# Cross network, six layers: GpSimd copies the corner weights of layers 1 to 5 behind the first half of layer 0 instead of ahead of it

## The chip, the cores and the metric

The kernel runs on one core of a Trainium2 chip. The metric is the device time in microseconds of one execution; of the kernel before there are three, 146.07, 146.46 and 146.69, median 146.46. A separate execution was profiled. The engines are named as in the profile: PE (matrix products), PEld (its weight loads), DVE (elementwise work, copies), ACT (activations, reads of PSUM), POOL (GpSimd), SP (issues DMAs).

## The reference

```python
# x0: 4096 x 416, ws: 6 x 416 x 416, bs: 6 x 416, all bf16
def reference(x0, ws, bs):
    x = x0
    for l in range(ws.shape[0]):
        x = x0 * (x @ ws[l] + bs[l]) + x
    return x
```

Each layer is a 4096 x 416 by 416 x 416 product, a bias, a product with the input and a sum. A layer needs the whole previous one.

## The kernel before, in words

**Layout.** The 416 features are cut into three blocks of 128 (k on the way in, m on the way out) and a remainder of 32. The 4096 rows of x are cut into two streams s of 2048, and each stream into four groups g of 512 columns. From layer 0 to layer 4 the activations stand transposed: XM[i] holds the three full blocks (128 partitions, 3, 4096), XR[i] the remainder, the four groups of a stream stacked in 4 x 32 partitions. XRx is XR of layer 0 with its two halves of 64 partitions swapped. XM[0] comes straight from DRAM by eight transposing DMAs (`load_x0t`, L78, one for each s and g). XR[0] is made on the chip: `load_xrem` (L83) loads rows into xrem, and `x0_rem` transposes them on DVE (L157), copies them into XR (L158) and into XRx (L161). x0_rem runs three times: for stream 0 it is cut in two halves of partitions, the first copied by DVE, the second (partitions 64 to 127, that is groups 2 and 3) by POOL; stream 1 is copied by DVE.

**Weights.** WM holds the rows of the three full blocks, WR the 32 remainder rows (four times, one for each group), WD the corner, remainder rows by remainder columns, laid out as four blocks of a diagonal, zero elsewhere. WD is zeroed by POOL and filled by `fill_wd(l0, l1)`: four POOL copies out of WR (L124). It is called for layer 0 and then for layers 1 to 5. WR of layers 1 to 5 comes by four DMAs of SP (L86).

**Order.** The program's order is written by hand, and each engine executes its own instructions in order. SP's queue holds, in order: the x transposes with the xrem loads among them, WM of layer 1, the four WR loads, WM of layers 2 to 5, X0rows, and later the transposes and stores of the end. Layer 0 is `first_layer(s)`, first s = 0, then s = 1. In it h = 0 (groups 0, 1) and h = 1 (groups 2, 3) come one after the other: 18 full products (L215), the remainder rows (`row`, L222, from XR or XRx), then for each m one tile of elementwise work (`ew_main`: ACT adds the bias out of PSUM, L166; DVE multiplies, L167, and adds, L168). The last part of stream 1 also makes the 32 remainder columns of both streams (`rem_first`: L192 with WD, L197 with WM, then ACT L172 and DVE L173 and L174, one remainder per stream).

Layers 1 to 4 go through six tiles (s, m). PE does 48 quarter products (L180) of the first tile, then the remainder rows of this and the next tile (`mm_row`, L186, which read the XR that the layer before has made), then the other tile's 48, and then, once per layer, `rem_pair`, both streams' remainder columns (L192, L197). Layer 5 is turned around, so that its result has rows on the partitions (L332, L341, L346), and is stored from there.

PSUM is handed out in four pairs of banks in turn (`two_banks`), and ACT's results go through six buffers t.

Of the kernel before, what the change touches and what calls it, by code (L numbers as in the profile page):

```python
# [16 lines left out]
def kernel(  # L17
# [9 lines left out]
    L = ws.shape[0]  # L27
# [42 lines left out]
    def col0(s, g):  # L70
        return SW * s + CW * g
# [50 lines left out]
    def fill_wd(l0, l1):  # L122
        for g in range(NG):
            nc.gpsimd.tensor_copy(WD[32 * g:32 * g + 32, l0:l1, g, :], WR[32 * g:32 * g + 32, l0:l1, NK * P:D])  # L124

    fill_wd(0, 1)
    fill_wd(1, L)

    PS = psum.tile([P, 8, CW], FP32)
    turn = [0]  # L130
# [1 line left out]
    def two_banks():  # L132
        i = 2 * (turn[0] % 4)
        turn[0] += 1
        return PS[:, i:i + 2, :]
# [20 lines left out]
    def x0_rem(s, p0, p1, eng):  # L156
        nc.vector.transpose(out=xrt[s][p0:p1], in_=xrem[s][p0:p1])  # L157
        eng.tensor_copy(XR[0][p0:p1, CW * s:CW * s + CW].rearrange("p (j t) -> p j t", t=16),  # L158
                              xrt[s][p0:p1].rearrange("p t j -> p j t"))
        for a in range(p0, p1, 64):  # L160
            eng.tensor_copy(XRx[s][64 - a:128 - a, :], XR[0][a:a + 64, CW * s:CW * s + CW])  # L161

    def ew_main(l, s, m, h, pt, cur, nxt):
        c0 = col0(s, 2 * h)
        t = tpool.tile([P, 2 * CW], BF16, name="t")
        nc.scalar.activation(t[:], pt.rearrange("p a b -> p (a b)"), ACT.Identity, bias=bM[:, m, l:l + 1], scale=1.0)  # L166
        nc.vector.tensor_tensor(out=t[:], in0=t[:], in1=XM[0][:, m, c0:c0 + 2 * CW], op=ALU.mult)  # L167
        nc.vector.tensor_tensor(out=nxt[:, m, c0:c0 + 2 * CW], in0=t[:], in1=cur[:, m, c0:c0 + 2 * CW], op=ALU.add)  # L168
# [40 lines left out]
    def first_layer(s):  # L209
        cur, nxt = XM[0], XM[1]  # L210

        def full(pt, m, h, gl, first, last):
            c0 = col0(s, 2 * h + gl)
            for k in range(NK):
                nc.tensor.matmul(pt[:, gl, :], lhsT=WM[:, 0, k, 128 * m:128 * m + 128], rhs=cur[:, k, c0:c0 + CW],  # L215
                                 start=(first and k == 0), stop=(last and k == NK - 1), skip_group_check=True)

        def row(pt, m, h, swapped, first):
            for gl in range(2):
                r0 = 32 * ((2 * h + gl + 2 * swapped) % 4)  # L220
                src = XRx[s][r0:r0 + 32, :] if swapped else XR[0][r0:r0 + 32, CW * s:CW * s + CW]
                nc.tensor.matmul(pt[:, gl, :], lhsT=WR[r0:r0 + 32, 0, 128 * m:128 * m + 128], rhs=src,  # L222
                                 start=first, stop=(not first), tile_position=(r0, 0), skip_group_check=True)

        pa = [two_banks() for m in range(NK)]
        if s == 0:
            for gl in range(2):
                for m in range(NK):
                    full(pa[m], m, 0, gl, True, False)
        else:  # L230
            for m in range(NK):
                for gl in range(2):
                    full(pa[m], m, 0, gl, True, False)
        pb = [two_banks()]
        row(pa[0], 0, 0, 0, False)
        row(pa[1], 1, 0, 1, False)
        row(pa[2], 2, 0, 0, False)
        if s == 1:
            row(pb[0], 0, 1, 0, True)
        if s == 0:  # L240
            x0_rem(0, 64, 128, nc.gpsimd)
        for m in range(NK):
            ew_main(0, s, m, 0, pa[m], cur, nxt)
        for gl in range(2):
            full(pb[0], 0, 1, gl, s == 0, s == 1)
        if s == 1:
            ew_main(0, s, 0, 1, pb[0], cur, nxt)
        for m in range(1, NK):
            pb.append(two_banks())
            for gl in range(2):  # L250
                full(pb[m], m, 1, gl, True, False)
        if s == 0:
            row(pb[0], 0, 1, 0, False)
            row(pb[2], 2, 1, 1, False)
            row(pb[1], 1, 1, 0, False)
            x0_rem(1, 0, 128, nc.vector)
            for m in range(NK):
                ew_main(0, s, m, 1, pb[m], cur, nxt)
        else:
            row(pb[1], 1, 1, 0, False)  # L260
            row(pb[2], 2, 1, 1, False)
            rem_first(pb)
# [16 lines left out]
    def rem_first(pb):  # L279
        pr2 = two_banks()  # L280
        for s in range(NS):
            mm_rem(0, s, pr2[:, s, :], XM[0], XR[0])
        for s in range(NS):
            ew_rem(0, s, pr2[:, s, :], XR[0], XR[1])
            ew_main(0, 1, 1 + s, 1, pb[1 + s], XM[0], XM[1])

    first_layer(0)
    first_layer(1)
    cur, curR = XM[1], XR[1]
    for l in range(1, LL):  # L290
# [136 lines left out]
```

## Time and profile before

| | before |
|---|---|
| timed, median of 3 | 146.46 us |
| the profiled execution's own time | 147.55 us |
| its span, first to last instruction | 145.7 us |
| PE busy | 126.2 us, 87% |
| DVE busy | 110.7 us, 76% |
| ACT busy | 83.9 us, 58% |
| POOL busy | 6.7 us, 5% |
| mean granted clock of PE | 0.946 |

The span leaves out 1.85 us around the first and last instruction. Busy shares are means over the whole span; the slices of the profile's page show that PE is at work nearly everywhere from slice 8 on and idle in slices 5 to 8 (some 15 to 29 us), and that its granted clock is low just there and a little beyond. Names in the rows: `t<-PS,bM` reads "writes t, reads PS and bM"; `x18` is a group of 18 merged instructions; a bracket gives the idle time before and what ended it.

### The profile page before, as it was taken

The numbers are of one execution on the slowest core, as the hardware profiler recorded it, in microseconds if no ns is written. First come the engines' busy times: TensorE is split into PE (matmuls) and PEld (weight loads), VectorE is DVE, ScalarE is ACT, GpSimd is POOL, SyncE is SP. The second block draws the span as 40 slices with busy tenths as digits, with TensorE's granted clock in tenths as the row PEclk, the third lists the DMA queues.
The fourth block names the chain that finished last, engine by engine and source line by source line (L and its number), as shares of the span: only waits on it lengthen the run. The fifth ranks groups of instructions, "written<-read, shape, count | busy, mean of one in ns | idle before, by whom it ended". The sixth has DMA issues, their size and how long they took to land.

```text
span 145.7 us, 3943 instructions
## 1 busy us (share of the span) xinstructions
PE 126.2 (87%) x1683; PEld 55.3 (38%) x1683; DVE 110.7 (76%) x196; ACT 83.9 (58%) x92; POOL 6.7 (5%) x20
## 2 busy tenths in 40 slices
PE   6999200199999999999999999999999999999960
PEld 2344000033444444444444445444444444455420
DVE  1256450064699989898988989898898999999990
ACT  1208000080968937759395686759584686675860
POOL 4200000600000000000000000000000120000000
PEclk9999985557999999999999999999999999999997
DMA  4999999999900000000000000000019798997553
GB/s 112 242 196 171 143 222 227 289 331 334 281 10 7 0 4 0 4 0 7 0 4 0 4 0 4 0 4 0 4 25 159 173 164 184 171 302 239 178 193 102
DMA packets 42021, 16.37 MB, mean 112 GB/s; under 512 B 30826, under 2 KB 42004, under 8 KB 42004
## 3 DMA queue, kind: packets, MB, share of 16 engines
q1 hardware_dynamic: 40504, 15.70, 49.3%
q10 hardware_dynamic: 1500, 0.42, 1.4%
q8 instruction: 13, 0.21, 0.6%
q14 instruction: 4, 0.03, 0.1%
HBM read 6.15 MB, written 3.41 MB: 66 GB/s over the span
## 4 chain that ended last, share of the span: by engine, by line
PE 75%; SPq 13%; DMA 4%; POOL 2%; DVE 1%; issue 1%; ACT 0%; DVEq 0%; POOLq 0%
PE PS L180 44%; SPq L78 11%; PE PS L332 11%; PE PS L215 7%; PE PS L186 4%; PE PS L197 4%; DMA WR<-in_ws_dram 4%; PE PS L192 2%; PE PS L341 1%; PE PS L222 1%; PE PS L346 1%; SPq L83 1%; DVE t L367 1%; POOL XR L158 1%; SPq L86 1%
## 5 line engine op out<-in xcount | busy, mean ns | idle before, releaser
L166 ACT ACTIVATE t<-PS,bM 128x1024 bf16<-128x1024 f32 x60 | 62.1, 1114 | 47.1 <-PE PS L222 25.8
L180 PE MATMUL PS<-XM,WM 128*32 128x512 bf16 x1152 | 65.2, 379 | 0.0
L167 DVE TENSOR_TENSOR t<-t,XM 128x1024 bf16<-128x1024 bf16 x60 | 41.5, 692 | 17.7 <-ACT t L166 17.7
L168 DVE TENSOR_TENSOR XM<-t,XM 128x1024 bf16<-128x1024 bf16 x60 | 41.8, 697 | 3.5
L180 PEld LDWEIGHTS <-WM 128*32 128x32 bf16 x1152 | 29.7, 97 | 33.8 <-issue 5.1
L215 PE MATMUL PS<-XM,WM 128*128 128x512 bf16 x72 | 18.9, 423 | 0.0
L332 PE MATMUL PS<-WM,XM 128*128 128x416 bf16 x96 | 17.9, 340 | 0.0
L222 PE MATMUL PS<-XR,WR 32*128 32x512 bf16 x16 | 2.8, 434 | 13.4 <-POOL XR L158 13.4
L356 ACT CAST t<-PS 128x832 bf16<-128x832 f32 x12 | 10.2, 852 | 5.0 <-PE PS L332 2.5
L332 PEld LDWEIGHTS <-XM 128*128 128x128 bf16 x96 | 8.9, 98 | 8.7 <-issue 2.2
L215 PEld LDWEIGHTS <-WM 128*128 128x128 bf16 x72 | 7.5, 107 | 11.2 <-issue 5.3
L197 PE MATMUL PS<-XM,WM 128*32 128x512 bf16 x120 | 8.2, 379 | 0.0
L172 ACT ACTIVATE t<-PS,bR 128x512 bf16<-128x512 f32 x10 | 6.8, 694 | 1.4 <-PE PS L197 1.4
L358 DVE TENSOR_TENSOR o<-t,XLrows 128x832 bf16<-128x832 bf16 x12 | 7.1, 592 | 0.5
L186 PE MATMUL PS<-XR,WR 32*128 32x512 bf16 x96 | 7.3, 379 | 0.0
L357 DVE TENSOR_TENSOR t<-t,X0rows 128x832 bf16<-128x832 bf16 x12 | 7.0, 584 | 0.0
L222 PEld LDWEIGHTS <-WR 32*128 32x128 bf16 x24 | 0.6, 93 | 15.6 <-issue 15.6
L139 PE MATMUL PS<-warm 128*128 128x512 bf16 (+1 forms) x12 | 5.1, 594 | 1.2 <-DVE warm L89 1.2
L276 POOL COPY XLrows<-scrR 128x512 bf16<-128x512 bf16 x2 | 1.4, 714 | 87.2 <-DMA scrR<-XR 87.2
L157 DVE STREAM_TRANSPOSE xrt<-xrem 64x512 bf16<-64x512 bf16 (+1 forms) x3 | 2.1, 708 | 3.6 <-DMA xrem<-in_x_dram 3.6
L174 DVE TENSOR_TENSOR XR<-t,XR 128x512 bf16<-128x512 bf16 x10 | 4.3, 426 | 0.8
L366 ACT CAST t<-PS 128x416 bf16<-128x416 f32 x8 | 4.0, 505 | 1.0 <-PE PS L332 0.8
(37 smaller groups left out, 40.6 us busy)
## 6 DMA issues: line engine op xcount, KB each, us to landing
X0rows<-in_x_dram SPq DMA_DIRECT2D x4, 832.0 KB, 10.0
out_dram<-o SPq DMA_DIRECT2D x12, 208.0 KB, 2.2
WM<-in_ws_dram SPq DMA_DIRECT2D x5, 312.0 KB
out_dram<-o SPq DMA_DIRECT2D x8, 104.0 KB, 2.0
WR<-in_ws_dram SPq DMA_DIRECT2D x4, 130.0 KB, 5.8
WM<-in_ws_dram ACTq DMA_DIRECT2D x1, 312.0 KB, 3.4
XM<-in_x_dram SPq DMA_TRANSPOSE x8, 4.7
xrem<-in_x_dram SPq DMA_DIRECT2D x1, 128.0 KB
```

The source lines that it names most:

```text
L78: nc.sync.dma_start_transpose(out=XM[0][:, :, c0:c0 + CW], in_=x0[c0:c0 + CW, 0:NK * P])
L166: nc.scalar.activation(t[:], pt.rearrange("p a b -> p (a b)"), ACT.Identity, bias=bM[:, m, l:l + 1], scale=1.0)
L167: nc.vector.tensor_tensor(out=t[:], in0=t[:], in1=XM[0][:, m, c0:c0 + 2 * CW], op=ALU.mult)
L168: nc.vector.tensor_tensor(out=nxt[:, m, c0:c0 + 2 * CW], in0=t[:], in1=cur[:, m, c0:c0 + 2 * CW], op=ALU.add)
L180: nc.tensor.matmul(pts[g // 2][32 * q:32 * q + 32, g % 2, :], lhsT=WM[:, l, k, 128 * m + 32 * q:128 * m + 32 * q + 32], rhs=cur[:, k, c0:c ...
L186: nc.tensor.matmul(pts[g // 2][:, g % 2, :], lhsT=WR[32 * g:32 * g + 32, l, 128 * m:128 * m + 128], rhs=curR[32 * g:32 * g + 32, CW * s:CW ...
L197: nc.tensor.matmul(pr[32 * g:32 * g + 32, :], lhsT=WM[:, l, k, NK * P:D], rhs=cur[:, k, c0:c0 + CW], start=False, stop=(k == NK - 1), tile ...
L215: nc.tensor.matmul(pt[:, gl, :], lhsT=WM[:, 0, k, 128 * m:128 * m + 128], rhs=cur[:, k, c0:c0 + CW], start=(first and k == 0), stop=(last ...
L332: nc.tensor.matmul(py[g // 2][:, g % 2, 0:D], lhsT=cur[:, k, q_cols(q, g)], rhs=WM[:, l, k, :], start=(first and k == 0), stop=((not first ...
L356: nc.scalar.copy(tv, py[h][:, :, 0:D])
L357: nc.vector.tensor_tensor(out=tv, in0=tv, in1=X0rows[:, b0:b0 + 5:4, :], op=ALU.mult)
L358: nc.vector.tensor_tensor(out=o[:], in0=tv, in1=XLrows[:, b0:b0 + 5:4, :], op=ALU.add)
```

## The change

The call `fill_wd(1, L)` is taken from its place right behind `fill_wd(0, 1)` and put between `first_layer(0)` and `first_layer(1)`. Since each engine executes in the order of the program, the four POOL copies now stand behind the two POOL copies that `x0_rem` makes inside `first_layer(0)`. All lines below the removed one are numbered one lower in the changed kernel until the inserted line: L158 becomes L157, L192 becomes L191.

```diff
     fill_wd(0, 1)
-    fill_wd(1, L)
 
     PS = psum.tile([P, 8, CW], FP32)
...
     first_layer(0)
+    fill_wd(1, L)
     first_layer(1)
```

On POOL, in the kernel before, from the fill of layer 0's corner on (32x5x32 are the copies of layers 1 to 5, the names behind "waits" are semaphores, DMAHW those of transfers):

```order
11 L124 COPY WD<-WR 32x32 [waits DMAHW4_49,Pool_49]
12 L124 COPY WD<-WR 32x32 [waits DVE_49] x3
13 L124 COPY WD<-WR 32x5x32 [waits DMAHW7_49]
14 L124 COPY WD<-WR 32x5x32 [waits DMAHW0_49]
15 L124 COPY WD<-WR 32x5x32 [waits DMAHW1_49]
16 L124 COPY WD<-WR 32x5x32 [waits DMAHW2_49]
17 L158 COPY XR_96<-xrt_89 64x512 [waits DVE_49,Pool_49]
18 L161 COPY XRx_91<-XR_96 64x512 [waits Pool_49]
```

The same place on POOL in the changed kernel:

```order
11 L124 COPY WD<-WR 32x32 [waits DMAHW4_49,Pool_49]
12 L124 COPY WD<-WR 32x32 [waits DVE_49] x3
13 L157 COPY XR_96<-xrt_89 64x512 [waits DVE_49,Pool_49]
14 L160 COPY XRx_91<-XR_96 64x512 [waits Pool_49]
15 L124 COPY WD<-WR 32x5x32 [waits DMAHW7_49]
16 L124 COPY WD<-WR 32x5x32 [waits DMAHW0_49,Pool_49]
17 L124 COPY WD<-WR 32x5x32 [waits DMAHW1_49]
18 L124 COPY WD<-WR 32x5x32 [waits DMAHW2_49]
```

The copies into XR and XRx, which wait for DVE alone, have moved ahead of the four that wait for transfers. PE's instructions stand in the same order as before; only its waits differ. At layer 1's `rem_pair` PE had, before:

```order
502 L180 MATMUL PS<-XM_94,WM 32x512
503 L192 LDWEIGHTS WD
504 L192 MATMUL PS<-XR_97,WD 32x512 [waits Activation_49]
505 L192 LDWEIGHTS WD
506 L192 MATMUL PS<-XR_97,WD 32x512
```

and has now:

```order
502 L179 MATMUL PS<-XM_94,WM 32x512
503 L191 LDWEIGHTS WD [waits Pool_49]
504 L191 MATMUL PS<-XR_97,WD 32x512 [waits Activation_49]
505 L191 LDWEIGHTS WD [waits Pool_49]
506 L191 MATMUL PS<-XR_97,WD 32x512
```

Each of the four weight loads out of WD waits for its POOL copy there. Layer 0's own weight loads out of WD wait for nothing new.

## Rows read from the trace of the kernel before

**Rows 1.** Timeline of PE: start us, duration us, instruction, [idle before <- releaser].

```profile
11.20 4.16 PE L215 MATMUL PS<-XM,WM 128*128 128x512 bf16 x18
28.72 0.61 PE L222 MATMUL PS<-XR,WR 32*128 32x512 bf16 x2 [13.36 <-POOL XR L158]
```

**Rows 2.** Timeline of POOL, the same columns, 25 to 30 us.

```profile
25.34 0.31 POOL L124 COPY WD<-WR 32x160 bf16<-32x160 bf16 x1 [18.29 <-DMA WR<-in_ws_dram]
...
27.26 0.32 POOL L124 COPY WD<-WR 32x160 bf16<-32x160 bf16 x1 [0.30 <-DMA WR<-in_ws_dram]
27.64 1.03 POOL L158 COPY XR<-xrt 64x512 bf16<-64x512 bf16 x1
28.73 0.61 POOL L161 COPY XRx<-XR 64x512 bf16<-64x512 bf16 x1
```

**Rows 3.** Chain of waits in order of time: start us, us, what.

```profile
11.44 2.07 SPq L78
...
17.14 1.79 SPq L78
...
36.73 3.99 PE PS L215 x18
40.72 0.33 PE PS L222 x4
...
42.89 2.59 PE PS L180 x48
45.48 0.54 PE PS L186 x8
```

**Rows 4.** The x transposes, line 78: issue to landing.

```profile
DMA to landing us min/median/max: 4.6/4.7/4.9
```

**Rows 5.** The WR loads, line 86: issue to landing.

```profile
DMA to landing us min/median/max: 5.7/5.8/6.0
```

**Rows 6.** Timeline of DVE, 10 to 48 us.

```profile
10.38 0.71 DVE L157 STREAM_TRANSPOSE xrt<-xrem 64x512 bf16<-64x512 bf16 x1 [0.91 <-DMA xrem<-in_x_dram]
...
18.16 0.71 DVE L157 STREAM_TRANSPOSE xrt<-xrem 128x512 bf16<-128x512 bf16 x1 [1.84 <-DMA xrem<-in_x_dram]
...
19.53 0.61 DVE L161 COPY XRx<-XR 64x512 bf16<-64x512 bf16 x2
...
37.70 0.69 DVE L167 TENSOR_TENSOR t<-t,XM 128x1024 bf16<-128x1024 bf16 x1 [3.11 <-ACT t L166]
...
43.01 0.42 DVE L173 TENSOR_TENSOR t<-t,XR 128x512 bf16<-128x512 bf16 x1
43.47 0.43 DVE L174 TENSOR_TENSOR XR<-t,XR 128x512 bf16<-128x512 bf16 x1
...
46.65 0.69 DVE L168 TENSOR_TENSOR XM<-t,XM 128x1024 bf16<-128x1024 bf16 x1
```

**Rows 7.** Windows: length, PE, PEld, DVE, ACT, POOL busy, PEclk, DMA share, GB/s.

```profile
15.40:20.00 4.60, 0.00 (x0) 0.00 (x0) 2.62 (x6) 0.00 (x0) 0.00 (x0) 1.00 0.91 138
20.00:22.00 2.00, 0.00 (x0) 0.00 (x0) 0.14 (x1) 0.00 (x0) 0.00 (x0) 0.69 1.17 258
...
34.00:36.00 2.00, 2.00 (x9) 0.74 (x7) 0.59 (x1) 0.00 (x0) 0.00 (x0) 0.90 1.13 336
```

**Rows 8.** Timeline of DVE in layer 4, 116 to 119 us.

```profile
116.32 1.10 DVE L167 TENSOR_TENSOR t<-t,XM 128x1024 bf16<-128x1024 bf16 x1
117.53 1.02 DVE L168 TENSOR_TENSOR XM<-t,XM 128x1024 bf16<-128x1024 bf16 x1
118.47 0.68 DVE L167 TENSOR_TENSOR t<-t,XM 128x1024 bf16<-128x1024 bf16 x1
```

**Rows 9.** Timeline of POOL in the same stretch.

```profile
116.06 0.82 POOL L276 COPY XLrows<-scrR 128x512 bf16<-128x512 bf16 x1 [86.72 <-DMA scrR<-XR]
117.39 0.61 POOL L276 COPY XLrows<-scrR 128x512 bf16<-128x512 bf16 x1 [0.51 <-DMA scrR<-XR]
```

**Rows 10.** DVE's waits from 45 us to the end: total us, times, longest.

```profile
DVE t L167 <- ACT t L166: 3.0, 10, 0.4
```

## The prediction

> **What bounds the kernel now.** I read the PE timeline first, because PE has the largest busy share and an idle stretch there is the first thing to price. In its two rows PE finishes 18 matmuls of layer 0 at 11.20 + 4.16 = 15.36 us, then stands still for 13.36 us until a GpSimd copy into XR (L158) is done [rows 1]. These are the remainder rows of stream 0's second half. The second view, POOL's timeline, says why that copy was late: it needs only the DVE transpose that ended at 10.38 + 0.71 = 11.09 [rows 6], but POOL executes in order, and ahead of it stand four copies into WD that wait for the WR transfers of layers 1 to 5; the last starts at 27.26, so the XR copy starts at 27.64 and XRx is ready at 28.73 + 0.61 = 29.34 [rows 2]. The third view, the chain, carries on from there on PE alone: first layer, then layer 1, whose remainder rows (L186) start at 45.48 [rows 3]. The fourth, the windows, shows the second price of the wait: the granted clock was 1.00 in 15.4 to 20.0 although PE did nothing, 0.69 in 20 to 22, and still 0.90 in 34 to 36, after work had resumed at 28.72 [rows 7]. 1.00 is the 2.4 GHz level; the lower one, 1.2 GHz, reads 0.50.
>
> From the chain view on, PE is never idle until the tail, so whatever moves the L186 at 45.48 moves the end, as long as DVE keeps up. I use that instruction as the milestone.
>
> **What the change does to POOL.** It removes nothing and adds nothing: four copies of 0.31 to 0.32 us [rows 2] go behind two copies (1.03 and 0.61). After it, XR's copy starts when DVE's transpose ends at 11.09, and both are done at about 11.1 + 1.03 + 0.61 + 0.1 = 12.8, some 2.6 us before PE wants them at 15.4. The 13.36 us wait goes whole. The four WD copies issue no DMA and are passed by no queue but POOL's; their transfers are issued by SP, whose order is untouched, so they stay where they are, at 25.3 to 27.6, plus what DVE costs them. The new order makes layer 1's corner matmuls (L191 of the changed kernel) wait for POOL. Behind them on PE stands all of layer 1; they come 3 us after the milestone, so they are late only if the copies are (first rival).
>
> **What is late next: PE's own path.** Matmuls at the full clock go at 3.99/18 = 0.222 us, the rows in 0.54 [rows 3].
> - Rows of stream 0, second half: 15.4 to 15.9.
> - Stream 1, first half, 18 matmuls. The fourth needs x columns whose transpose SP issues at 11.44; these transposes land 4.6 to 4.9 us after issue [rows 4], so at 16.3, before 15.9 + 0.67 = 16.6. No wait; done at 15.9 + 3.99 = 19.9.
> - Its rows need DVE's XRx copies, ended at 19.53 + 0.61 = 20.14 [rows 6]: 20.2 to 20.7.
> - Second half: three matmuls to 21.4, then the last transpose, issued at 17.14 [rows 3], at 22.0; I have no row of its own landing. Fifteen more: 22.0 + 3.33 = 25.3.
> - Rows and corner remainder 42.89 - 40.72 = 2.17, to 27.5; then 48 matmuls of layer 1, 2.59, to 30.1. Layer 1's weights are issued at 17.14 + 1.79 = 18.93; their landing too is unshown, and by WR's 5.7 to 6.0 [rows 5] it is an estimated 24.9, early enough. WR itself is there at 27.2.
>
> So PE could reach the milestone at 30.1. It had the low clock for part of that work before; now its longest pause is under 1 us, so I take the full clock.
>
> **DVE's path is longer by a little.** The milestone reads stream 0's remainder of layer 0, which DVE makes. DVE waits for the second xrem transfer until 18.16, which no part of the change touches, and ends its layout copies at 20.14. Behind them stand three tiles of stream 0 (four took 43.01 - 37.70 = 5.31, so 1.33 each, 3.98), then the piece that ran from 37.70 to 43.47 + 0.43 = 43.90, 6.20 [rows 6]. ACT feeds these in time: past 45 us, where DVE works at the same pace, it waited for ACT 3.0 us in all [rows 10]. Sum: 20.14 + 3.98 + 6.20 = 30.32, with a handover 30.4. DVE ends the wait, not PE. Without any disturbance the milestone moves from 45.48 to 30.4: 15.1 us.
>
> **The disturbance.** Before, DVE was idle while POOL copied into WD; now DVE is in its multiply and add tiles. The only rows with both at work are near the end: two POOL copies of 0.82 and 0.61 [rows 9] lie beside a multiply of 1.10 and an add of 1.02, where the next multiply has 0.68. That tile took 118.47 - 116.32 = 2.15 instead of 1.33 [rows 8], so 0.82 for 1.43 us of copies, 0.57 per us. For 4 x 0.315 = 1.26 us this is 0.72. The bounds are 0, if the copies fall between, and 0.41 per copy whatever its length, 1.64. I take 0.72, since the copies are short. The earlier pair at 11 to 13 us costs nothing: DVE waits for xrem anyway (1.84 us idle before 18.16).
>
> The Trainium skill speaks of this under "SBUF — State Buffer", section "SBUF: two separate sides": GpSimd and a VectorE instruction with two SBUF inputs lock one shared pair of ports for a whole instruction, and the other one waits entirely. By that the four copies could cost 1.26 and the gain would be 13.8; the trace agrees that DVE is stretched, though by 0.41 beside a copy of 0.82.
>
> Milestone: 30.4 + 0.72 = 31.1, a shift of 45.48 - 31.1 = 14.4. Is DVE then able to follow? It ends layer 0 at 46.65 + 0.69 = 47.34 before, 3.44 after the remainder's end, so at 30.32 + 0.72 + 3.44 = 34.5 now. PE needs this for stream 1's corner remainder of layer 1, at 31.1 + 0.54 + 2.59 + 0.92 = 35.2 (0.92 is stream 0's half of 2.17 - 0.33): spare 0.7. DVE's shift is 12.8, so it trails PE by 1.6 more than before, and it has 3.0 us of waiting for ACT left in ten pieces up to the end [rows 10] to catch up in. PE therefore keeps the 14.4.
>
> **Sum.** The profiled execution took 147.55 us, span 145.7 and 1.85 around it; it lies 1.09 above the median of 146.46. 147.55 - 14.4 = 133.15 for it, and 146.46 - 14.4 = 132.1 for the median, which I predict. The forecast's own range: port cost 0 gives 131.4, port cost 1.64 gives 146.46 - 13.4 = 133.1; with half a us for run to run and small waits, 130.8 to 133.6.
>
> **Rivals.**
> - POOL is locked out. From 18.16 on DVE works almost without a pause; if the WD copies get in only when it stops, PE meets its new wait at 30.4 + 0.54 + 2.59 = 33.5. DVE finishes what it has: layer 0 at 33.8 and four tiles, 39.1; then four copies, about 1.3 to 1.9. PE goes on at 40.7, 7.2 late: 146.46 - 15.1 + 7.2 = 138.6. For it: DVE's chain above has no gap. Against it: at 116.06 and 117.39 POOL's copies did run beside DVE's tiles and took 0.82 and 0.61 [rows 8, 9]. 6%. The skill's exclusive lock on that page is the rule from which such a lockout would come.
> - A transfer takes the wait's place. Everything PE asked for after 28 us had long landed, so late landings don't show in the waits. Were the last transpose as late as WR (27.2), the milestone would come at 27.2 + 3.33 + 2.17 + 2.59 = 35.3, 4.2 later: 136.3. Against it: transposes have landed in 4.6 to 4.9. 8%, spread between 133 and 137.
> - Slower than before: the clock. The small waits on x could leave PE at half rate from about 21 us on, as it was in 22 to 34 before. Each us of full-speed work then costs one more, so from 14.4 us of such work on, some 8 us into layer 1, the kernel is slower than before; 20 us of it would give 146.46 - 14.4 + 20 = 152.1. Against it: the clock stayed 1.00 through 4.6 us of idleness and was back at 0.90 in 34 to 36, within 8 us of the work's return at 28.72 [rows 1, 7]. 2%.
> - The order on POOL does not matter, as XR would be held up by another wait on its way, its time staying at 146.5. Its only input was there at 11.09. 2%.
>
> **Chances.** The forecast has 82%. The range 130.8 to 134.8 holds it and part of the transfer case. About 0.5% of the time, 0.7 us, is what a measurement can tell from no change: faster 0.96 (forecast, lockout, transfer), same 0.02, slower 0.02.
>
> **What would show it.** Right: XR's POOL copy starts near 11.2; no PE wait above 1.5 us before layer 1; the granted clock stays 1.00 in 15 to 35; DVE runs gapless from 18.2 to beyond 34; the first L185 stands near 31 and is released by DVE's remainder add; the tiles beside the WD copies are stretched by 0.7 in sum. Wrong: an L191 of layer 1 released by POOL (lockout), an L214 released by a DMA for more than 1 us (transfer), clock under 0.9 after 20 (clock), or idle PE in layers 2 to 4, which would mean that DVE did not catch up.

## The result and the profile after

| | before | changed |
|---|---|---|
| timed, median | 146.26 us (145.95 to 146.69, 4 runs) | 132.75 us (132.46 to 132.90, 4 runs) |
| ratio to before | | 0.907, 95% interval 0.904 to 0.910 |
| profiled execution, its span | 147.55, 145.7 us | 132.90, 131.1 us |
| PE busy, mean granted clock | 126.2 us, 0.946 | 122.8 us, 0.991 |
| DVE busy | 110.7 us | 111.2 us |
| POOL busy | 6.7 us | 8.3 us |

The changed kernel is 13.5 us faster by the medians and 14.65 by the two profiled executions. The profiled execution of before is a slow one: it lies 1.29 us above this median, at a mean clock (0.946) that its fast runs have too (0.943 to 0.964 in the sets below), so the 14.65 is not the gain of the median. POOL's timeline of the changed kernel answers to [rows 2]:

```profile
11.21 1.03 POOL L157 COPY XR<-xrt 64x512 bf16<-64x512 bf16 x1 [4.29 <-DVE xrt L156]
12.31 0.96 POOL L160 COPY XRx<-XR 64x512 bf16<-64x512 bf16 x1
25.03 0.31 POOL L124 COPY WD<-WR 32x160 bf16<-32x160 bf16 x1 [11.77 <-DMA WR<-in_ws_dram]
25.83 2.29 POOL L124 COPY WD<-WR 32x160 bf16<-32x160 bf16 x3 [0.49 <-DMA WR<-in_ws_dram]
```

XR's copy starts at 11.21 instead of 27.64 and waits for DVE, its only input. The WD copies stand where they stood (25.03 for the first, 25.34 before), but three of them fill 2.29 us. PE's timeline, against [rows 1]:

```profile
12.61 3.40 PE L214 MATMUL PS<-XM,WM 128*128 128x512 bf16 x14 [1.20 <-DMA XM<-in_x_dram]
15.94 0.39 PE L221 MATMUL PS<-XR,WR 32*128 32x512 bf16 x2
...
27.35 2.76 PE L179 MATMUL PS<-XM,WM 128*32 128x512 bf16 x48
30.84 0.61 PE L185 MATMUL PS<-XR,WR 32*128 32x512 bf16 x8 [0.73 <-DVE XR L173]
...
33.98 0.39 PE L191 MATMUL PS<-XR,WD 128*32 128x512 bf16 x4
```

The 13.36 us wait for POOL is gone. What is left are 1.20 us for an x transpose and 0.73 for DVE's remainder add ahead of the first L185; layer 1's L191, which now waits for POOL too, has no idle time before it. The first L185 stood at 45.48 before [rows 3], so it moved by 14.64, and the span shrank by 14.6: nothing was given back later. DVE's timeline, against [rows 6], shows the new pace maker:

```profile
11.63 1.16 DVE L166 TENSOR_TENSOR t<-t,XM 128x1024 bf16<-128x1024 bf16 x1 [0.55 <-ACT t L165]
12.83 0.98 DVE L167 TENSOR_TENSOR XM<-t,XM 128x1024 bf16<-128x1024 bf16 x1
...
18.44 0.71 DVE L156 STREAM_TRANSPOSE xrt<-xrem 128x512 bf16<-128x512 bf16 x1 [1.97 <-DMA xrem<-in_x_dram]
...
25.81 0.68 DVE L166 TENSOR_TENSOR t<-t,XM 128x1024 bf16<-128x1024 bf16 x1
26.53 0.69 DVE L167 TENSOR_TENSOR XM<-t,XM 128x1024 bf16<-128x1024 bf16 x1
27.14 0.80 DVE L166 TENSOR_TENSOR t<-t,XM 128x1024 bf16<-128x1024 bf16 x1
...
30.36 0.42 DVE L173 TENSOR_TENSOR XR<-t,XR 128x512 bf16<-128x512 bf16 x1
```

From the second xrem transpose at 18.44 to the remainder add's end at 30.78 no row of DVE carries an idle time. The windows (columns as in [rows 7]) show that the clock no longer falls in this stretch. First one of before, where it read 0.50, then those of the changed kernel:

```profile
28.00:34.00 6.00, 5.22 (x16) 1.70 (x16) 3.39 (x6) 3.12 (x3) 1.27 (x2) 0.50 1.11 331
```

```profile
20.00:22.00 2.00, 1.87 (x15) 0.51 (x14) 1.90 (x5) 1.10 (x2) 0.00 (x0) 1.00 1.14 253
...
28.00:34.00 6.00, 5.27 (x100) 2.37 (x96) 5.83 (x11) 4.72 (x6) 0.12 (x1) 1.00 1.11 331
34.00:36.00 2.00, 2.00 (x44) 1.01 (x40) 1.97 (x4) 2.00 (x4) 0.00 (x0) 1.00 1.11 333
```

One caution on the chain view after. It names a transfer as what came before a DVE multiply:

```profile
22.22 6.36 DMA WM<-in_ws_dram
...
28.59 0.69 DVE t L166
```

That multiply reads no weights, and DVE came to it straight from the add before it. The link is inferred, and wrong; the timeline of DVE corrects it.

### The profile page after: what moved, and what is told of

It is laid out like the page before. It is cut to its first block, busy times and chain, and to the rows that moved or that the text cites. A ratio compares the mean times of both kernels' runs of the same rounds, so it can differ in the third digit from the quotient of the medians.

```text
span 131.1 us, 3942 instructions
## 1 busy us (share of the span) xinstructions
PE 122.8 (94%) x1681; PEld 54.5 (42%) x1683; DVE 111.2 (85%) x196; ACT 84.0 (64%) x92; POOL 8.3 (6%) x20
## 4 chain that ended last, share of the span: by engine, by line
PE 72%; SPq 16%; DMA 5%; DVE 3%; issue 1%; ACT 0%; DVEq 0%
PE PS L179 46%; SPq L78 13%; PE PS L332 12%; PE PS L185 5%; DMA WM<-in_ws_dram 5%; PE PS L196 4%; PE PS L341 2%; SPq L86 1%; PE PS L191 1%; PE PS L346 1%; SPq L83 1%; DVE t L367 1%; SPq L74 1%; DVE o L370 1%; DVE t L166 1%
## 5 line engine op out<-in xcount | busy, mean ns | idle before, releaser
L166 DVE TENSOR_TENSOR t<-t,XM 128x1024 bf16<-128x1024 bf16 x60 | 42.1, 702 | 2.4 <-ACT t L165 2.4
L179 PEld LDWEIGHTS <-WM 128*32 128x32 bf16 x1152 | 29.7, 97 | 33.8 <-issue 5.1
L214 PE MATMUL PS<-XM,WM 128*128 128x512 bf16 x70 | 16.4, 379 | 1.4 <-DMA XM<-in_x_dram 1.2
L214 PEld LDWEIGHTS <-WM 128*128 128x128 bf16 x72 | 6.8, 97 | 10.6 <-issue 3.2
L185 PE MATMUL PS<-XR,WR 32*128 32x512 bf16 x96 | 7.3, 379 | 0.7 <-DVE XR L173 0.7
L196 PEld LDWEIGHTS <-WM 128*32 128x32 bf16 x120 | 3.2, 97 | 3.2
L102 DVE COPY WR<-WR 32x416 bf16<-32x416 bf16 x3 | 0.8, 260 | 4.4 <-DMA WR<-in_ws_dram 4.3
```

The lines of the kernel that those rows point to most:

```text
L179: nc.tensor.matmul(pts[g // 2][32 * q:32 * q + 32, g % 2, :], lhsT=WM[:, l, k, 128 * m + 32 * q:128 * m + 32 * q + 32], rhs=cur[:, k, c0:c ...
L185: nc.tensor.matmul(pts[g // 2][:, g % 2, :], lhsT=WR[32 * g:32 * g + 32, l, 128 * m:128 * m + 128], rhs=curR[32 * g:32 * g + 32, CW * s:CW ...
L196: nc.tensor.matmul(pr[32 * g:32 * g + 32, :], lhsT=WM[:, l, k, NK * P:D], rhs=cur[:, k, c0:c0 + CW], start=False, stop=(k == NK - 1), tile ...
```

## The experiments

The runs come in three sets; those of one set share a chip and the runs of the kernel before. Before had a median of 145.39 (144.77 to 147.04) in the first, 146.02 (144.79 to 146.95) in the second and 145.78 (145.07 to 147.82) in the third, 11 runs each.

### POOL's order alone: DVE makes the copies (first set)

```diff
 # kernel before
-            x0_rem(0, 64, 128, nc.gpsimd)
+            x0_rem(0, 64, 128, nc.vector)
```

> The kernel before with one word changed: the second half of stream 0's remainder is copied into XR and XRx by DVE instead of POOL; the four WD copies of layers 1 to 5 stay in their old place. Theory (PE waited only because XR's copy stood behind WD's on POOL): PE's 13.4 us wait goes as fully as in the changed kernel, since DVE has the 0.9 us for the two copies free ahead of its xrem wait; 132.4 to 133.1 us, first L186 of layer 1 at 30.5 to 31.1. Rival (the gain hangs on something else that moving the WD copies does, such as when they read WR): the time stays near 146.

Measured: 132.30 us (132.11 to 132.44), ratio to before 0.908 (0.903 to 0.913), a little below the 132.4 to 133.1 expected, as is the first L186 at 30.19 (30.5 to 31.1 expected). PE's and POOL's rows, in the line numbers of before:

```profile
30.19 0.61 PE L186 MATMUL PS<-XR,WR 32*128 32x512 bf16 x8 [1.00 <-DVE XR L174]
```

```profile
23.53 0.31 POOL L124 COPY WD<-WR 32x160 bf16<-32x160 bf16 x1 [16.52 <-DMA WR<-in_ws_dram]
24.77 1.97 POOL L124 COPY WD<-WR 32x160 bf16<-32x160 bf16 x3 [0.93 <-DMA WR<-in_ws_dram]
```

With the WD copies in their old place on POOL and XR's copy off POOL, the same time is reached: the changed kernel's ratio is 0.907 (0.904 to 0.910). So the gain comes from XR's copy no longer standing behind WD's; anything else that the move does is within the half per cent of these intervals.

### The clock's share: fillers in the wait (first and second set)

```diff
 # kernel before, first_layer(0); 60 and 54 matmuls
         if s == 0:
+            for i in range(60):
+                nc.tensor.matmul(PS[:, 4, :], lhsT=warm[:, 0:P], rhs=warm[:], start=True, stop=True, skip_group_check=True)
             row(pb[0], 0, 1, 0, False)
```

> The kernel before with 60 more matmuls of 512 columns on constant data (result unused) ahead of the remainder rows for which PE waits; the wait on POOL stays. It prices the clock alone. Theory: the granted clock stays 1.00, the rows still start at 28.7 to 29.4, and PE's work from 29.4 to 45.5 shrinks to 0.33+3.99+0.54+3.99+2.17+2.59 = 13.6, so the first L186 comes at 43.0, 2.5 earlier, and the profiled execution at 145.0; since nothing is left that varies with the clock, the timed runs agree with the profiled one, 144.6 to 145.2. Rival A (the profiled execution of before lies 1.1 above its median for another reason): the median is 146.3 - 2.5 = 143.8. Rival B (low clock cost nothing): 146.3.

> The kernel before with 54 instead of 60 filler matmuls ahead of the remainder rows that wait for POOL. With 60 the fillers themselves ended at 28.0, after XRx at 27.9, so they ended the wait. With 54 they end near 26.9, PE waits some 1 us for POOL again, with the granted clock at 1.00. Theory: from XRx's end to the first L186 13.9 to 14.0 us instead of the 16.1 of before, so the low clock costs 2.1 to 2.2 us; time 143.2 to 144.3, at or below the 144.2 of the 60. Rival (the low clock is worth only the 1.2 us by which the 60 fillers changed the median): equal to 144.2 or above.

Measured: 144.23 us (143.91 to 144.29) with 60 and 144.33 (143.69 to 145.37) with 54; ratios to before 0.990 (0.984 to 0.995) and 0.990 (0.984 to 0.996). With 60 the fillers were still running when XR was ready: the rows started at 28.03 without a wait, while XR's copy had ended at 26.22 + 1.04 = 27.26. So the 60 spoil part of what they show. With 54, PE waits for POOL again, and the clock is 1.00 (PE timeline, then windows):

```profile
28.94 0.39 PE L222 MATMUL PS<-XR,WR 32*128 32x512 bf16 x2 [1.70 <-POOL XR L158]
...
43.22 0.61 PE L186 MATMUL PS<-XR,WR 32*128 32x512 bf16 x8
```

```profile
22.00:28.00 6.00, 5.24 (x25) 2.25 (x23) 0.00 (x0) 0.00 (x0) 1.39 (x5) 1.00 1.15 243
28.00:34.00 6.00, 4.79 (x28) 1.95 (x31) 3.38 (x6) 3.12 (x3) 1.49 (x2) 1.00 1.11 332
```

From the rows' start to the first L186 are 43.22 - 28.94 = 14.28 us. The same timeline of before has that row at

```profile
45.41 0.61 PE L186 MATMUL PS<-XR,WR 32*128 32x512 bf16 x8
```

which is 45.41 - 28.72 = 16.69 us behind its rows [rows 1]. The low clock cost 2.4 us in the profiled execution of before, where 2.1 to 2.2 were expected. By the medians the fillers gain 1.69, interval 0.5 to 2.4, so whether the timed runs pay the same is left open within that: the 144.33 lies just outside the theory's 143.2 to 144.3 and fits its rival (144.2 or above), and only the trace decides for the theory. The expectation's theory for the 60 (144.6 to 145.2) missed: it took the profiled execution's arrival of WR (XR's copy at 27.64, here at 26.22), which is the next point.

### Whom the kernel before waits for: WR earlier (second set)

```diff
 # kernel before, SP's queue
+    for g in range(NG):
+        load_wr(nc.sync, g, 1, L)
     load_x0t(1, 2)
     load_x0t(1, 3)
     load_wm(nc.sync, 1)
-    for g in range(NG):
-        load_wr(nc.sync, g, 1, L)
```

> The kernel before with SP's four WR loads issued ahead of stream 1's last two x transposes instead of behind layer 1's weights; POOL's order is as before. Theory (the kernel before hands on the landing of WR one for one, through POOL's order): WR is issued 5.4 us earlier and lands 5 to 5.5 us earlier, so XR's copy on POOL and PE's rows come 5 to 5.5 us earlier, and the clock falls for a shorter time or not at all; 138.5 to 141 us. Rival (POOL's own start, the x transposes or layer 1's weights release PE): 144 or more.

Measured: 139.92 us (139.34 to 140.01), ratio 0.958 (0.953 to 0.964). PE's timeline, then POOL's:

```profile
21.46 0.61 PE L222 MATMUL PS<-XR,WR 32*128 32x512 bf16 x2 [5.91 <-POOL XR L158]
...
37.29 0.61 PE L186 MATMUL PS<-XR,WR 32*128 32x512 bf16 x8
```

```profile
20.00 0.32 POOL L124 COPY WD<-WR 32x160 bf16<-32x160 bf16 x1 [0.20 <-DMA WR<-in_ws_dram]
20.39 1.03 POOL L158 COPY XR<-xrt 64x512 bf16<-64x512 bf16 x1
```

POOL's order is as before, and XR's copy comes 27.64 - 20.39 = 7.25 us earlier because WR does, more than the 5 to 5.5 expected, since WR also landed 3.4 us after its issue instead of 5.7 to 6.0 [rows 5]. The span is 8.2 shorter (137.5); most of the rest is the stretch from the rows to the first L186, 37.29 - 21.46 = 15.83 against 16.69. So the kernel before hands on WR's arrival to its end. That arrival differs between executions: XR's copy began at 27.64 in the profile of before, 26.22 with the 60 fillers and 27.86 with the 54, in which nothing ahead of it on POOL is changed.

### The changed kernel again, as a base (second and third set)

> The changed kernel once more, as the base for the other runs of this call. 132.3 to 132.9 us; first L185 of layer 1 released by DVE's remainder add after a PE wait of 0.5 to 1.1 us. If the kernel before varies more from execution to execution than this one, because it alone hands on how late the WR transfers land, its times spread over 1.5 to 2.3 us in this call and these over less than 0.8.

> The changed kernel as the base for the other two runs of this call, on the same chip: 131.7 to 132.9 us, PE's wait for DVE ahead of the first L185 0.5 to 1.1 us.

Measured: 132.09 us (131.70 to 132.52; 132.3 to 132.9 expected) and 132.12 (131.69 to 132.65), 6 runs each; ratios 0.905 (0.900 to 0.910) and 0.906 (0.903 to 0.910). PE's wait for DVE ahead of the first L185 was 1.03 and 0.68. The spread is 0.8 and 1.0 us, that of before 2.2 and, without its longest run, 1.9 in the same sets. That is what a kernel that no longer waits for WR would show, but not proof: before has more runs, and the kernel with WR earlier, which still waits for it, spread over 0.7 in four.

### What the WD copies cost DVE: left out (first and third set)

```diff
 # changed kernel
     first_layer(0)
-    fill_wd(1, L)
     first_layer(1)
```

> The changed kernel without the four WD copies of layers 1 to 5 (WD stays zero there, so the corner products are left out of the result). It prices what these copies cost DVE. Theory from the trace after: DVE loses some 0.2 us beside them (its path from the second xrem transpose to the remainder add took 12.34 instead of 12.16), so the first L185 comes 0.1 to 0.3 earlier and the time is 132.4 to 132.7. Rival (the predicted 0.72 was right and is hidden in the trace): 132.0. Rival (PE's new wait in layer 1 for POOL costs something): PE's idle time ahead of L191 of layer 1 in the changed kernel goes here, and the time falls by as much.

> The changed kernel without the four WD copies of layers 1 to 5 (their corner products are left out of the result), now beside the base on one chip. Theory (these copies cost DVE 0.15 to 0.36 us, as the paths of 12.35 to 12.56 against 12.20 say): 0.1 to 0.5 us under the base. Rival (the predicted 0.72): 0.7 or more under it.

Measured: 131.72 us (131.51 to 132.15) without a base beside it, below all that was expected, and 132.10 (131.57 to 132.40) beside the base's 132.12, where 0.1 to 0.5 less were expected. The medians show no difference, and with spreads of 0.8 to 1.0 us they can't show one of 0.2. The trace is sharper. From the second xrem transpose's start to the end of stream 0's remainder add, DVE took 12.20 us without the copies in both profiles, and 12.34, 12.55 and 12.44 in the three profiles of the changed kernel: 0.14 to 0.35 more, on average 0.24. These are DVE's rows without them:

```profile
17.25 0.71 DVE L156 STREAM_TRANSPOSE xrt<-xrem 128x512 bf16<-128x512 bf16 x1 [1.14 <-DMA xrem<-in_x_dram]
...
29.03 0.42 DVE L173 TENSOR_TENSOR XR<-t,XR 128x512 bf16<-128x512 bf16 x1
```

The predicted 0.72 is out. PE had no idle time ahead of layer 1's L191, with or without the copies, so the new wait for POOL costs nothing.

### Whether DVE sets the pace: xrem earlier, and off SP (first and second set)

```diff
 # changed kernel, first variant
+    load_xrem(nc.sync, 1, 0, 128)
     load_x0t(1, 1)
-    load_xrem(nc.sync, 1, 0, 128)
 # changed kernel, second variant: both loads of SP's queue go to ACT's
     load_xrem(nc.scalar, 0, 0, 64)
+    load_xrem(nc.scalar, 0, 64, 128)
+    load_xrem(nc.scalar, 1, 0, 128)
```

> The changed kernel with the second stream's xrem load issued by SP one place earlier, ahead of stream 1's second x transpose. Theory (DVE's path from the second xrem landing decides when layer 1's remainder rows start): xrem lands 2 us earlier, at about 16.4, DVE starts its layout copies at 16.5 behind stream 0's first tiles, and the remainder add is done near 28.9; PE's own path, 30.1, then decides, and PE's 0.73 us wait ahead of the first L185 goes: L185 at 30.1 to 30.3, 132.0 to 132.2 us. Rival (PE's path decides, through the x transposes, and the wait for DVE is only its shadow): unchanged or up to 0.6 later, since the second transpose of stream 1 moves 0.6 back: 132.7 to 133.3.

> The changed kernel with the two xrem loads of SP's queue moved to ACT's queue, right behind the first one. Theory (after the change the first layer is paced by what SP issues one after the other: the x transposes for PE, the second xrem for DVE): the last x transpose is issued 1.3 us earlier, near 15.8, and lands near 20.6; the second xrem is there before DVE has finished stream 0's first tiles at 16.5; first L185 at 28.9 to 29.5 and 131.0 to 131.6 us. Rival (the DMA engines, whose busy share is 0.9 to 1.3 in 4 to 16 us, are the limit and not SP): the 64 byte rows of xrem go ahead of the x transposes, stream 0 starts later by their time, and the total is 132.3 to 134.

Measured, first variant: 132.65 us (132.16 to 133.11), ratio to before 0.911 (0.906 to 0.916), no base in its set. PE's timeline:

```profile
17.49 3.40 PE L214 MATMUL PS<-XM,WM 128*128 128x512 bf16 x15 [0.68 <-DMA XM<-in_x_dram]
...
30.12 0.61 PE L185 MATMUL PS<-XR,WR 32*128 32x512 bf16 x8
```

The wait for DVE is gone, as the theory says, and the first L185 stands at the 30.1 of PE's own path; but PE pays 0.68 for the transpose that was moved back, as the rival says, and the time does not fall. Second variant: 131.91 us (131.71 to 131.96) beside 132.09, not the 131.0 to 131.6 expected. Again DVE is early and PE late, now at its start:

```profile
8.93 2.10 PE L214 MATMUL PS<-XM,WM 128*128 128x512 bf16 x9 [0.84 <-DMA XM<-in_x_dram]
...
29.81 0.61 PE L185 MATMUL PS<-XR,WR 32*128 32x512 bf16 x8
```

So the two paths, DVE's through xrem and PE's through the x transposes, lie about a microsecond apart (PE waits 0.68 to 1.03 us in the three profiles of the changed kernel), and moving a transfer trades one for the other.

### A version meant to beat both: a tile into DVE's idle time (third set)

```diff
 # changed kernel, first_layer(0)
-            x0_rem(1, 0, 128, nc.vector)
             for m in range(NK):
                 ew_main(0, s, m, 1, pb[m], cur, nxt)
+                if m == 0:
+                    x0_rem(1, 0, 128, nc.vector)
```

> The changed kernel with DVE's layout copies for stream 1 placed behind the first tile of stream 0's second half instead of ahead of all three. Theory (DVE stands idle 1.5 to 2.0 us for the second xrem with a tile ready behind it, and its path decides when layer 1's remainder rows start): the tile fills the idle time, the copies start at 18.1 to 18.4 instead of 17.9, two tiles instead of three stand behind them, the remainder add is done 0.8 to 1.1 us earlier, PE's wait ahead of the first L185 falls to 0 to 0.3, and the time is 0.6 to 1.0 us under the base. Rival (PE's rows of stream 1, which wait for these copies, are what matters): they start 0.3 later, and the time is equal to the base within 0.3.

Measured: 131.37 us (131.01 to 132.06) beside the base's 132.12, 0.75 less; ratio to before 0.902 (0.898 to 0.906) against the base's 0.906 (0.903 to 0.910). DVE's timeline, then PE's:

```profile
17.00 0.69 DVE L166 TENSOR_TENSOR t<-t,XM 128x1024 bf16<-128x1024 bf16 x1 [0.38 <-ACT t L165]
...
18.33 0.70 DVE L156 STREAM_TRANSPOSE xrt<-xrem 128x512 bf16<-128x512 bf16 x1
...
29.01 0.42 DVE L173 TENSOR_TENSOR XR<-t,XR 128x512 bf16<-128x512 bf16 x1
```

```profile
21.70 3.40 PE L214 MATMUL PS<-XM,WM 128*128 128x512 bf16 x15 [0.30 <-DMA XM<-in_x_dram]
...
29.79 0.61 PE L185 MATMUL PS<-XR,WR 32*128 32x512 bf16 x8
```

The tile takes the place of DVE's wait for xrem, the stretch from the transpose to the remainder add shrinks to 29.43 - 18.33 = 11.10, and PE no longer waits for DVE. In the two profiles the first L185 moves only from 30.00 to 29.79, since PE's own path decides now, and the span by 0.3. The intervals of the two ratios overlap as well, so the mechanism is shown, but not that it is worth the 0.75.

## Why the prediction was right, and where it was off

The predicted 132.1 us lies 0.65 below the first median, inside the range, and on the medians of the two later sets. That last is luck: there the kernel before was faster too (146.02 and 145.78, against the 146.46 that the prediction started from), and the gain was 13.9 and 13.7, not 14.4.

**What goes, and what is late next.** Right. The wait goes whole, XR's copy starts at 11.21 (predicted 11.1 to 11.2), the clock stays 1.00, and DVE's remainder add ends the next wait at 30.78, for L185 at 30.84 (predicted 31.1). That DVE really set the pace there, and was not only the neighbouring row, is shown by the runs that gave it time (xrem earlier, xrem off SP, a tile first): in each PE's wait for it went away.

**PE's own path.** 30.1 predicted, 27.35 + 2.76 = 30.11 measured, with one difference inside: PE waited 1.20 us, until 12.61, for an x transpose. The prediction had no pause above 1 us; in [rows 1] PE needed these columns at 11.20 + 0.67 = 11.87 and had no wait. The transposes landed later here than the 4.6 to 4.9 us after issue of [rows 4]:

```profile
DMA to landing us min/median/max: 4.7/4.8/5.4
```

In the other two profiles of the changed kernel the same wait was 0.36 and 0.17. The clock stayed at 1.00 through it, and the delay was caught up: PE was 0.6 behind the predicted times at 16.48, 0.3 at 21.01 and not at all at 25.3, since the predicted path had 0.6 us of waiting for the last transpose in it.

**The disturbance by POOL.** Mis-sized: 0.72 predicted from the only pair of rows at hand [rows 8, 9], 0.24 measured. The price was taken by the copy's length, 0.57 per us, and that is not what decides; what decides is which of the two starts first. Two of the copies by themselves:

```profile
25.83 0.83 POOL L124 COPY WD<-WR 32x160 bf16<-32x160 bf16 x1 [0.49 <-DMA WR<-in_ws_dram]
27.45 0.67 POOL L124 COPY WD<-WR 32x160 bf16<-32x160 bf16 x1
```

Each started while a DVE multiply ran, and ended at 26.66 and 28.12, 0.17 and 0.18 after that multiply (26.49 and 27.94). So POOL does the waiting. DVE loses only what is left of the copy: the adds right behind these two multiplies kept their 0.69, and only the multiply at 27.14, which starts ahead of the end of the add before it, took 0.80 instead of 0.68. In [rows 8, 9] it was DVE that came second, to copies that had already begun, and there it paid 0.41 and 0.33. That the milestone was hit within 0.3 is in part luck: the disturbance was 0.48 smaller than predicted, and the second xrem came 0.28 later (18.44 against 18.16).

**DVE catching up.** Right: after 32 us it waited for ACT 1.8 us in seven pieces, where before there were 3.0 in ten [rows 10], and PE was busy without a gap from 34 us on.

**From the profiled execution to the median.** This is the step that was off by most. I took 14.4 us, worked out in one execution of before, from the median of others. The profiled pair moved by 14.65, the medians by 13.5, 13.9 and 13.7. The kernel before hands on how late WR lands, and in the execution that I read it landed late: that execution lay 1.09 us above the median, as I wrote, and the change removes just that lateness too. It should have been taken off the gain: 146.46 - 14.4 + 1.09 = 133.15, a gain of 13.3. The run with WR earlier shows the mechanism; that the whole 1.09 was WR is argued, not shown, from the 1.6 us by which XR's copy differs between profiles and from the profile with 54 fillers, where XR's copy was as late (27.86) and which lay 1.04 above its median.

**The rivals.** POOL was not locked out: all four WD copies were done at 28.1, 6 us ahead of layer 1's L191. Under "SBUF — State Buffer", section "SBUF: two separate sides", the Trainium skill has the one that starts first hold the shared ports for its whole instruction while the other waits; the rows agree, as the one that started second ended its own time, less 0.13 to 0.15 us, after the first. But such waiting did not add up to a lockout: over 12 us of DVE work without a pause every copy got in when the DVE tile that ran at its start had ended. The transfers cost PE 1.20 us in one place, which is the prediction's own sign of that rival (an L214 released by a DMA for more than 1 us), though also inside what it allowed the forecast (no wait above 1.5). It did not delay the milestone, as PE still waited 0.73 us for DVE ahead of it. The clock and the case of no effect are out.

## What to carry to other kernels

A copy that waits for a late transfer delays everything behind it on its in-order engine, even on an engine that is 5% busy: look at what stands ahead of the late instruction, not at the engine's load. When such a wait goes, price the clock that it had let fall as well, and work out the path of every engine to the same milestone, since the next one was only about a microsecond behind. And a gain read in one execution must be set against that execution alone: if the wait that goes varies from run to run, the part by which this execution lay above the median is no gain of the median.

## What the runs showed of the hardware that was not expected

- Of a POOL copy and a DVE tile with two inputs, the one that starts second pays: in these rows it ends its own time, less 0.13 to 0.15 us, after the end of the first. XR's copy ended at 12.24 and the multiply that began beside it at 12.79 (0.69 alone); XRx's copy, begun beside that multiply, ended at 13.27 (0.61 alone); the add, begun beside XRx's copy, at 13.81 (0.69 alone). So against DVE work without a pause the small copies do the waiting (0.31 became 0.67 to 0.83), and DVE loses 0.12 at most to each.
- The same transfers in the same queue order arrive up to 1.6 us apart from one execution to the next, at the end of some 25 us of loading, as XR's copies behind them show (26.22 to 27.86). The kernel that waits for the last of them spread over 1.9 to 2.2 us (10 and 11 runs), the one that does not over 0.8 to 1.0 (6 runs); that the first causes the second is likely, not shown.
